# A two-branch attention kernel: products of the first branch by exact pieces of heads, narrower denominators, and a last half row in two quarters

## The chip, the cores and the metric

The kernel runs on one core of a Trainium2 chip. The metric is device time in microseconds (us): 316.14 us as the median of 3 runs (315.89 to 316.18). Engines are named as the profile names them: PE (matrix products) and PEld (its weight loads), DVE (vector), ACT (scalar functions), POOL (the general engine), SP (which mostly issues DMAs).

## The reference

Two attention branches over the same 2048 x 640 input are mixed by a gate for each token. There are 32 heads of 20 columns.

```python
g = sigmoid((x * gate_w).sum(-1, keepdims=True))
# branch A: linear attention, per head h (Dh = 20)
q, k, v = split(x @ wqkv)
phi(t)  = concat(softmax(t @ w_phi[h]), softmax(-(t @ w_phi[h])))      # 40 features
kv, z   = phi(k)^T v, sum over tokens of phi(k)
a       = (phi(q) kv / (phi(q) z + 1e-6)) @ wo
# branch B: softmax attention within 4 segments of 512 tokens (lower triangle), with a
# memory M, z carried from segment to segment; o = sig(beta) * memory + (1 - sig(beta)) * softmax part
b       = o @ wo_B
return g * a + (1 - g) * b
```

## The kernel before

Everything below has an order written out by hand for all engines: the emission order in the code is the order of each engine's queue. Tokens go in 16 chunks of 128 (`ch` or `sc`, 0 to 15), the 640 columns of a projection in KC = 5 blocks `j` of 128. A block of 128 columns doesn't end where a head of 20 does: heads 6, 12, 19 and 25 lie across two blocks.

The stages, in order of time:

1. Start, to about 9 us. The weight for keys of branch A is multiplied by the feature weight `w_phi`: `emit_foldT` turns block `ic` of the natural weight into `WkT`, and `emit_foldM` (L183) multiplies it by `Wphi`, a table that holds, for each block `j`, the feature weights of the heads `TH[j]`, each masked to the rows of the block that belong to the head. `emit_Wphi` builds the five tables on DVE and POOL. ACT copies each result to `WkA`.
2. Keys and values of branch A, to about 52 us: for each chunk `pk`, its two exponentials (`Ek`), the sums and reciprocals (`ksum`, `krec`), the normalized features `EkSn` (POOL, and DVE for the last), and `vA`.
3. The fold of the query weight (`WqA`, again `emit_foldM`, five times) at 53 to 57 us, then `kv` (L391) for each block `j`, which `emit_kvn` masks and writes into `kvn`, and the sums `z` by additions on DVE. `kvd` holds for each block two columns a head: the sum's entries, and ones of the mask.
4. Queries of branch A, 61 to 88 us: `emit_pq` makes `pq` and ACT the two exponentials `Eq` (signs `sgn` 0 and 1) in two halves `qb` of 1024 tokens. `emit_first_den` makes the denominators of chunks 0 to 3.
5. The products, 88 to 126 us. A loop over chunks and signs takes 32 groups. `emit_num` (L471) makes one group in a PSUM tile of two banks (heads 0 to 15 and 16 to 31), from one of three buffers taken in turn: `nps[(2 * ch + sgn) % 3]`. `PIECES` lists its matmuls as (block j, bank, first head, last head + 1); all of a group's matmuls write into one tile, where those in `FIRST` open a bank and those in `LAST` close it. DVE multiplies the group by the reciprocal sums (`emit_tt`, L524), POOL adds the two signs (L683, `oA`, from `tt` tiles of which there are two), and SP turns the sum for the output projection. Between groups PE runs one half projection of branch B (`emit_half`, L606, matmuls at L554, evicted by ACT at L613). Where `ch % 4 == 1` for chunks 1, 5 and 9, `emit_den` (L489) makes the denominators of two chunks behind each sign's group, 20 matmuls, in free columns of the same tile; DVE reads them at L500 and L501, and from there on POOL prepares the next four chunks' factors (L515, L517).
6. Branch B, 126 to 303 us: bursts of scores (L754), exponentials on ACT (`PT`, L758), triangles on POOL (L765), products with V (L808), with the remaining projections and the output products spread among them by `PLAN`.
7. The end, from 303 us: the output rows of chunks 12 to 15, in halves of 320 columns called (n, half). `fill` (L1058) and `turned_mm` multiply the turned blocks by WoB; `evict` (L1108) either adds the row so far on DVE (for halves in `SUMMED`) or copies on ACT, and issues the output DMA named in `out_to`. The half (2, 1) comes last: it takes the bank of half (0, 0) when ACT has copied that one, and has five matmuls, an add on DVE and a DMA on SP.

The groups in PSUM are opened by the first matmul of a bank; later matmuls of the same bank write columns that nothing has written since, or add to those that something has.

The lists that the change replaces:

```python
TH = [(0, 12), (6, 13), (12, 25), (19, 26), (25, 32)]
PIECES = [(0, 0, 0, 12), (2, 0, 12, 16), (2, 1, 16, 25), (4, 1, 25, 32),
          (1, 0, 6, 13), (3, 1, 19, 26)]
FIRST, LAST = {0, 2}, {4, 5}
HW = 13
```

Blocks 0 and 2 are taken over heads to which they have no rows (7 to 11, and 20 to 24), where their tables hold zeros. In columns a group is 240, 80, 180, 140, 140 and 140, in all 920.

Of the kernel before, what the change touches and what calls it, by code (L numbers as in the profile page):

```python
# [8 lines left out]
ALU = mybir.AluOpType  # L9
# [6 lines left out]
def kernel(  # L16
# [15 lines left out]
    nc = tc.nc  # L32
    P = 128
    S = 2048
    D = 640
    H = 32
    DH = 20
    KC = D // P
# [7 lines left out]
    out2 = out[0]  # L46
# [10 lines left out]
    bd01 = const.tile([P, 4], F32, name="bd01")  # L57
    EPS_HI = 1.0 / 2 ** 20 + 3.0 / 2 ** 26
    epsm = const.tile([P, 4], F32, name="epsm")
    TH = [(0, 12), (6, 13), (12, 25), (19, 26), (25, 32)]  # L60
    PIECES = [(0, 0, 0, 12), (2, 0, 12, 16), (2, 1, 16, 25), (4, 1, 25, 32),
              (1, 0, 6, 13), (3, 1, 19, 26)]
    FIRST, LAST = {0, 2}, {4, 5}
    HW = 13

    gS = res.tile([P, NCH], F32, name="gS")
    omgS = res.tile([P, NCH], F32, name="omgS")
# [31 lines left out]
    for what in "w1 w3 x0 g v0 v1".split():  # L99
        n = int(what[1:]) if len(what) > 1 else 0  # L100
# [17 lines left out]
    for g in range(3):  # L118
# [16 lines left out]
                            compare_op=ALU.is_ge, fill=0.0, base=DH - 1, channel_multiplier=-1)  # L135
    wmw = Aw.tile([P, KC, HW], F32, name="wmw")
    nc.gpsimd.memset(wmw, 0.0)
    Wphi = wq_hold.tile([P, KC, HW, DH], BF16, name="Wphi")
    kvn = Aw.tile([P, 2, KC, HW, DH], BF16, name="kvn")
    kvd = Aw.tile([P, 2, KC, H, 2], BF16, name="kvd")  # L140
    for j, (h0, h1) in enumerate(TH):
        nc.gpsimd.tensor_copy(out=wmw[:, j, 0:h1 - h0], in_=wmask[:, j, h0:h1])
    def emit_Wphi(j, eng):
        h0, h1 = TH[j]
        eng.tensor_tensor(out=Wphi[:, j, 0:h1 - h0, :],
                                in0=Wc[:, j:j + 1, :].to_broadcast([P, h1 - h0, DH]),
                                in1=wmask[:, j, h0:h1, None].to_broadcast([P, h1 - h0, DH]),
                                op=ALU.mult)

    for j, eng in ((0, nc.vector), (4, nc.gpsimd), (2, nc.vector), (1, nc.gpsimd), (3, nc.gpsimd)):  # L150
        emit_Wphi(j, eng)
    for sgn in range(2):
        nc.gpsimd.memset(kvn[:, sgn], 0.0)
# [10 lines left out]
    for row, val in ((DH, EPS_HI), (DH + 1, 1e-6 - EPS_HI)):  # L164
        nc.gpsimd.affine_select(out=epsm, in_=epsm, pattern=[[-32, 4]], compare_op=ALU.not_equal,
                                fill=val, base=-row, channel_multiplier=1)
# [6 lines left out]
    def w2tile(name):  # L173
        return aps.tile([P, 2, 512], F32, name=name, tag="w2")
# [8 lines left out]
    def emit_foldM(WT, dst, ic, eng=nc.scalar.copy):  # L183
        ps = w2tile("fold_ps")
        for n, (j, bk, lo, hi) in enumerate(PIECES):
            h0 = TH[j][0]
            nc.tensor.matmul(ps[:, bk, (lo - 16 * bk) * DH:(hi - 16 * bk) * DH],
# [129 lines left out]
    for step in "T0a T2d M0a T1d M2a T4d M1a T3d X0 M4a M3a k0 g k1 v0 v1 r0 r1".split():  # L317
        n = int(step[1:2] or 0)
# [26 lines left out]
    for n in range(KC):  # L345
# [12 lines left out]
        out=xg, in0=vA[:, :, 0, 320].rearrange("p (g u) -> p u g", u=4)[:, :, :, None].to_broadcast([P, 4, 4, 4]),  # L358
        in1=bd01[:, None, None, :].to_broadcast([P, 4, 4, 4]), op=ALU.mult)
# [42 lines left out]
    def emit_kvn(j):  # L402
        h0, h1 = (P * j) // DH, (P * j + P - 1) // DH + 1
        g0 = TH[j][0]
        nc.vector.tensor_tensor(
# [24 lines left out]
    for what in "z4 f0 g0 f1 f2 f3 g1 l0 l1 n0 n1 z1 g2 l2 n2 z1 g3 l3 n3 q0 f4 g4 l4 z9 n4 h0 e0".split():  # L430
        j = int(what[1:])
# [31 lines left out]
    WoB = WvA.rearrange("p c b n -> p (c b n)")[:, 0:KC * D].rearrange("p (c n) -> p c n", c=KC)  # L463
# [7 lines left out]
    def emit_num(ch, sgn):  # L471
        qb, qc = divmod(ch, HB // P)
        t = nps[(2 * ch + sgn) % 3].tile([P, 2, 512], F32, name="num")
        for n, (j, bk, lo, hi) in enumerate(PIECES):
            h0 = TH[j][0]
            nc.tensor.matmul(t[:, bk, (lo - 16 * bk) * DH:(hi - 16 * bk) * DH],  # L476
# [12 lines left out]
    def emit_den(t, ch):  # L489
        qb, qc = divmod(ch, HB // P)  # L490
        for sgn in range(2):
            for j in range(KC):
                nc.tensor.matmul(t[:, sgn].rearrange("p h e -> p (h e)"),  # L493
                                 lhsT=Eqs[qb, j][:, sgn, qc * P:(qc + 1) * P],
                                 rhs=kvd[:, sgn, j].rearrange("p h e -> p (h e)"),
                                 start=(j == 0), stop=(j == KC - 1))

    def emit_rr(rr, uu, t, o, n):
# [73 lines left out]
    def emit_first_den():  # L572
        for n in range(NB):
            emit_den(dt[:, n], n)
# [67 lines left out]
    def emit_num_at(i):  # L642
        if i < len(order):
            ch, sgn = order[i]
            t = nums[ch, sgn] = emit_num(ch, sgn)
            if ch % 4 == 1 and ch < NCH - 4:
                for n in range(2):
                    emit_den(den_view(t)[:, n], ch + 3 + 2 * sgn + n)
# [6 lines left out]
    for ch in range(NCH):  # L655
# [4 lines left out]
        for sgn in range(2):  # L660
            t = nums.pop((ch, sgn))
# [12 lines left out]
            if (ch, sgn) in EXPS:  # L674
                part = EXPS[ch, sgn]
                nc.scalar.activation(out=(phiks[1][:, 0] if part == "k" else phiq_st)[:, :, 0:DH],
                                     in_=stages[part][0][:, :, 0:DH], func=ACT.Exp)
            if (ch, sgn) in TWICE:
                emit_next_half()
            if ahead and k == 2 and sgn == 0:  # L680
# [3 lines left out]
                                in0=tt[:, 0], in1=tt[:, 1], op=ALU.add)  # L684
# [19 lines left out]
    with ExitStack() as bctx:  # L704
# [11 lines left out]
        def st_tile():  # L716
            st_pools.append(st_pools.pop(0))
            return st_pools[-1].tile([P, 2, L], F32, name="st_ps")

        oBs, ogs = {}, {}  # L720
        nda = bnd.tile([P, 2, 512], F32, name="nda")
# [140 lines left out]
        oTs, rows = {}, {}  # L862
# [112 lines left out]
        oT4 = oTA[:, 0:4]  # L975
# [42 lines left out]
        first = NCH - 4  # L1018
        oB = oBs[NSEG - 1]
        pair_ps = [st_tile() for _ in range(2)]  # L1020
        banks = {(n, half): pair_ps[n][:, half, 0:320] for n in range(2) for half in range(2)}

        def row_mm(n, half):
            nc.tensor.matmul(banks[n, half], lhsT=ident_b,
                             rhs=rows[first + n][:, half * 320:(half + 1) * 320], start=True, stop=False)
# [27 lines left out]
                tdv = td[:, :, ji].rearrange("p n (j i) d -> p n j i d", j=2)  # L1053
                nc.vector.tensor_tensor(out=oview[:, j:j + 2], in0=tdv[:, 0], in1=tdv[:, 1], op=ALU.add)

        SUMMED = {(0, 1), (1, 1), (3, 0), (2, 1)}

        def fill(n, half, k5s):  # L1058

            own = (n, half) not in SUMMED  # L1060
            if own:
                row_mm(n, half)
            for k5 in k5s:
                nc.tensor.matmul(banks[n, half], lhsT=oT4[:, n, k5, :],
                                 rhs=WoB[:, k5, half * 320:(half + 1) * 320],
                                 start=(k5 == 0 and not own), stop=(k5 == KC - 1))
# [28 lines left out]
        def last_tr(n):  # L1095
# [7 lines left out]
        last_tr(3)  # L1103
        nc.scalar.copy(out=oT4[:, 2:4, 4, :], in_=tp[:, 2:4])
        out_to = {(0, 1): (nc.sync, 0, 0), (1, 1): (nc.sync, 1, 0), (2, 0): (nc.sync, 2, 0),
                  (3, 1): (nc.scalar, 3, 0), (2, 1): (nc.sync, 2, 320)}

        def evict(n, half):  # L1108
            row = rows[first + n][:, half * 320:(half + 1) * 320]
            if (n, half) in SUMMED:  # L1110
                nc.vector.tensor_tensor(out=row, in0=banks[n, half], in1=row, op=ALU.add)
            else:
                nc.scalar.copy(out=row, in_=banks[n, half])
            if (n, half) in out_to:
                eng, n, lo = out_to[n, half]
                hs = slice(lo, (half + 1) * 320)
                eng.dma_start(out=out2[(first + n) * P:(first + n + 1) * P, hs], in_=rows[first + n][:, hs])

        both = ((0, 0), (0, 1), (1, 0), (1, 1)), ((2, 0), (3, 0), (3, 1))
# [4 lines left out]
            turned_mm(n, half, (4,))  # L1124
        for n, half in both[0]:
            evict(n, half)
        banks[2, 1] = pair_ps[0][:, 0, 0:320]
        fill(2, 1, range(KC))
        for n, half in both[1] + ((2, 1),):
            evict(n, half)  # L1130


# [28 lines left out]
```

## Time and profile before

| what | value |
|---|---|
| median of 3 runs | 316.14 us (315.89 to 316.18) |
| the profiled execution's own time | 315.77 us |
| its span, first to last instruction | 314.1 us |
| granted PE clock | 1.000 |
| PE busy | 304.0 us, 97% |
| ACT busy | 252.2 us, 80% |
| DVE busy | 223.7 us, 71% |
| POOL busy | 209.0 us, 67% |
| matmuls | 4014, each with a weight load |

The profile is of one execution, and its durations stand against that execution's time; the 1.67 us between span and time lie outside the instructions. A busy time is the sum of what an engine's instructions took. A matmul's duration there includes the way through the array (a matmul of 64 columns shows 0.193 us, though the next starts 0.029 us later), so what a matmul costs in a row of matmuls is read from start to start, which is how the chain of waits counts it. The chain follows what ended last back through its releasers, so an engine can carry the chain all through a stage and still be tied with another one.

### The profile page before, as it was taken

How to read it: one execution, taken by the hardware profiler on the slowest of the kernel's cores; microseconds unless marked ns; L12 is line 12 of the kernel's file. 1: busy time of each engine (PE TensorE's matmuls, PEld its weight loads, DVE VectorE, ACT ScalarE, POOL GpSimd, SP SyncE). 2: the span in 40 equal slices, each digit the busy share in tenths (PEclk: the TensorE clock that was granted, in tenths of full speed). 3: DMA queues.
4: the chain of work that ended last, by engine and by line, in shares of the span. 5: the costliest groups of instructions: out<-in, count | busy, mean ns of one | idle time of the engine just before them, and what ended most of it. 6: DMA issues, size and time to landing. Idle time of an engine off the chain costs nothing.

```text
span 314.1 us, 9759 instructions
## 1 busy us (share of the span) xinstructions
PE 304.0 (97%) x4014; PEld 208.3 (66%) x4014; DVE 223.7 (71%) x507; ACT 252.2 (80%) x320; POOL 209.0 (67%) x308
## 2 busy tenths in 40 slices
PE   8999999999999999999999999999999999999995
PEld 7788877755578888465566666665656666665673
DVE  3487997999779997568767586877755765445463
ACT  4677888277845648999998999999998898998953
POOL 8788599004247989856657477878786877666550
DMA  7988934439137979755221583386653453222132
GB/s 208 211 183 201 220 97 135 120 105 366 57 19 139 140 111 140 152 93 89 51 55 33 69 144 64 74 111 68 88 107 76 90 93 73 66 75 55 45 92 84
DMA packets 94006, 34.55 MB, mean 110 GB/s; under 512 B 82442, under 2 KB 93834, under 8 KB 93962
## 3 DMA queue, kind: packets, MB, share of 16 engines
q1 hardware_dynamic: 93386, 33.28, 52.6%
q10 hardware_dynamic: 576, 0.66, 0.8%
q8 instruction: 31, 0.51, 0.7%
q14 instruction: 13, 0.11, 0.1%
HBM read 6.10 MB, written 2.62 MB: 28 GB/s over the span
## 4 chain that ended last, share of the span: by engine, by line
PE 73%; ACT 22%; DMA 2%; issue 1%; DVE 1%; ACTq 0%; DVEq 0%
ACT PT L758 19%; PE st_ps L754 9%; PE proj L884 9%; PE proj L940 9%; PE pk L240 7%; PE pq L418 7%; PE proj L554 7%; PE pv L240 7%; PE nda L808 6%; PE num L476 4%; PE kv_ps L391 2%; DMA wnat_k<-in_A_wqkv_dram 2%; PE num L493 1%; PE nda L816 1%; ACT ek L912 1%
## 5 line engine op out<-in xcount | busy, mean ns | idle before, releaser
L758 ACT ACTIVATE PT<-st_ps 128x1024 bf16<-128x1024 f32 x160 | 153.7, 1023 | 12.7 <-PE st_ps L754 10.4
L765 POOL TENSOR_SCALAR_AFFINE_SELECT PT<-PT 128x512 bf16<-128x512 bf16 (+1 forms) x130 | 87.0, 688 | 45.7 <-ACT PT L758 45.4
L808 PEld LDWEIGHTS <-PT 128*128 128x128 bf16 x1280 | 40.0, 96 | 9.5 <-issue 5.6
L808 PE MATMUL nda<-vB,PT 128*128 128x21 bf16 x1240 | 41.6, 173 | 0.1
L259 POOL TENSOR_TENSOR EkSn<-Ek,krec 128x1280 bf16<-128x1280 bf16 x15 | 35.1, 2360 | 7.9 <-DVE krec L258 6.0
L946 DVE CAST Z<-proj 128x320 bf16<-128x320 f32 x44 | 21.1, 488 | 23.5 <-PE proj L940 22.4
L940 PEld LDWEIGHTS <-xTf 128*128 128x128 bf16 x300 | 26.4, 97 | 14.2 <-issue 5.7
L425 ACT ACTIVATE Eq<-pq 128x1024 bf16<-128x1024 f32 x20 | 19.4, 1021 | 12.0 <-PE pq L418 12.0
L255 DVE TENSOR_REDUCE ksum<-Ek 128x64 f32<-128x1280 bf16 x16 | 23.6, 1475 | 7.2 <-ACT Ek L251 7.2
L524 DVE TENSOR_TENSOR tt<-num,rr 128x640 f32<-128x640 f32 x32 | 25.0, 814 | 4.5 <-POOL rr L517 1.7
L884 PE MATMUL proj<-WkA,oTA 128*128 128x320 bf16 x160 | 28.2, 300 | 0.0
L683 POOL TENSOR_TENSOR oA<-tt 128x640 bf16<-128x640 f32 x16 | 24.6, 1541 | 5.2 <-DVE tt L524 5.0
L754 PE MATMUL st_ps<-Z 32*128 32x512 bf16 (+3 forms) x256 | 24.7, 299 | 3.2 <-ACT PT L758 2.3
L251 ACT ACTIVATE Ek<-pk 128x640 bf16<-128x640 f32 x32 | 20.8, 703 | 7.9 <-PE pk L240 6.8
L754 PE MATMUL st_ps<-Eq 32*128 32x512 bf16 (+3 forms) x256 | 25.1, 299 | 1.9 <-ACT PT L758 1.3
L240 PEld LDWEIGHTS <-xTf 128*128 128x128 bf16 x200 | 22.6, 113 | 4.7
L848 POOL TENSOR_TENSOR oB<-td 128x320 bf16<-128x320 f32 x22 | 19.0, 861 | 5.0 <-DVE td L845 5.0
L418 PE MATMUL pq<-xTf,WqA 128*128 128x512 bf16 x100 | 22.2, 379 | 0.0
L884 PE MATMUL proj<-WvA,oT 128*128 128x320 bf16 x120 | 21.0, 300 | 0.0
L845 DVE TENSOR_TENSOR td<-nda,rec 128x640 f32<-128x640 f32 x23 | 19.0, 825 | 2.5 <-DVE rec L835 0.5
L554 PEld LDWEIGHTS <-xTf 128*128 128x128 bf16 x180 | 16.2, 97 | 4.6
L884 PEld LDWEIGHTS <-oTA 128*128 128x128 bf16 x160 | 13.6, 97 | 8.0 <-issue 4.0
(178 smaller groups left out, 554.2 us busy)
## 6 DMA issues: line engine op xcount, KB each, us to landing
Z<-EkSn SPq DMA_DIRECT2D x32, 160.0 KB, 2.9
out_dram<-orow SPq DMA_DIRECT2D x8, 160.0 KB, 1.8
out_dram<-oTA SPq DMA_DIRECT2D x6, 160.0 KB, 1.8
WvA<-in_A_wqkv_dram SPq DMA_DIRECT2D x2, 400.0 KB, 6.3
WvB<-in_B_wv_dram SPq DMA_DIRECT2D x1, 800.0 KB, 4.7
WkB<-in_B_wk_dram SPq DMA_DIRECT2D x1, 800.0 KB, 6.5
WqB<-in_B_wq_dram SPq DMA_DIRECT2D x1, 800.0 KB, 8.2
WkA<-in_A_wo_dram SPq DMA_DIRECT2D x1, 800.0 KB, 9.9
```

The costliest lines, as they stand in the source:

```text
L240: nc.tensor.matmul(ps[:, bk, 0:n], lhsT=key_tokens(c, sc), rhs=rhs, start=(c == 0), stop=(c == by_row[-1][0] if sc == 0 and W is WkA else ...
L259: (nc.vector if sc == NCH - 1 else nc.gpsimd).tensor_tensor(out=EkSn[:, sc].rearrange("p s (h f) -> p (s h) f", f=DH), in0=Ek.rearrange("p ...
L418: nc.tensor.matmul(pq[:, half, :], lhsT=WqA[:, c, j * P:(j + 1) * P], rhs=xq[:, 2 * qb + half, c], start=(c == 0), stop=(c == KC - 1))
L524: nc.vector.tensor_tensor(out=tt[:, sgn].rearrange("p (b h) d -> p b h d", b=2), in0=ps, in1=csb, op=ALU.mult)
L554: nc.tensor.matmul(ps, lhsT=xq[:, sc // 4, cc, sc % 4 * P:(sc % 4 + 1) * P], rhs=W[:, cc, half * 320:(half + 1) * 320], start=(cc == 0), s ...
L683: nc.gpsimd.tensor_tensor(out=oA.rearrange("p (h d) -> p h d", d=DH), in0=tt[:, 0], in1=tt[:, 1], op=ALU.add)
L754: nc.tensor.matmul(ps[:, i - i0, o:o + L - c * P], lhsT=kT[32 * i:32 * i + 32, c * P:(c + 1) * P], rhs=qT[32 * i:32 * i + 32, c * P:L], st ...
L758: nc.scalar.activation(out=PT[:, i0:i0 + 2], in_=ps, func=ACT.Exp, scale=SCALE_B)
L765: nc.gpsimd.affine_select(out=v, in_=v, pattern=[[0, n_i], [1, P]], compare_op=ALU.is_ge, fill=0.0, base=0, channel_multiplier=-1)
L808: nc.tensor.matmul(nd[:, j, i], lhsT=block(st, c)[:, i, (j - c) * P:(j - c + 1) * P], rhs=vB[:, c, 4 * st.g + i, :], start=(c == 0), stop= ...
L884: nc.tensor.matmul(ps, lhsT=oT[:, k % KC], rhs=W[:, k % KC, hs], start=(k == 0), stop=(k == n - 1))
L940: nc.tensor.matmul(ps, lhsT=xq[:, sc // 4, k, sc % 4 * P:(sc % 4 + 1) * P], rhs=W[:, k, half * 320:(half + 1) * 320], start=(k == 0), stop ...
```

## The change

Three things:

1. `TH` is now the heads that have rows in block `j`: (0, 7), (6, 13), (12, 20), (19, 26), (25, 32). `PIECES` has ten pieces in order of blocks, with the shared heads 6, 12, 19 and 25 as pieces of their own where a second block adds to them, and a block that reaches over head 16 cut there. A group has ten matmuls of 140, 20, 120, 20, 60, 80, 20, 120, 20 and 120 columns, in all 720. The tables `Wphi`, `kvn` and `wmw` are 8 heads wide and not 13, which makes the memsets and products that fill them smaller, and the tables of `Wphi` are built in order of blocks.
2. In `emit_den` block 0 still writes all 32 heads (64 columns), and blocks 1 to 4 write only their own heads: 14, 16, 14 and 14 columns.
3. Half (2, 1) is no longer filled and evicted as a whole. Its columns 320 to 479 go to the bank of half (0, 0) and 480 to 639 to that of half (1, 0), in five matmuls of 160 columns each; after the other evictions DVE adds the two quarters, and one DMA on SP writes out columns 320 to 639 as before.

```diff
-    TH = [(0, 12), (6, 13), (12, 25), (19, 26), (25, 32)]
-    PIECES = [(0, 0, 0, 12), (2, 0, 12, 16), (2, 1, 16, 25), (4, 1, 25, 32),
-              (1, 0, 6, 13), (3, 1, 19, 26)]
-    FIRST, LAST = {0, 2}, {4, 5}
-    HW = 13
+    TH = [(P * j // DH, (P * j + P - 1) // DH + 1) for j in range(KC)]
+    PIECES = [(0, 0, 0, 7), (1, 0, 6, 7), (1, 0, 7, 13), (2, 0, 12, 13), (2, 0, 13, 16),
+              (2, 1, 16, 20), (3, 1, 19, 20), (3, 1, 20, 26), (4, 1, 25, 26), (4, 1, 26, 32)]
+    FIRST, LAST = {0, 5}, {4, 9}
+    HW = 8
...
-    for j, eng in ((0, nc.vector), (4, nc.gpsimd), (2, nc.vector), (1, nc.gpsimd), (3, nc.gpsimd)):
+    for j, eng in ((0, nc.vector), (1, nc.gpsimd), (2, nc.vector), (3, nc.gpsimd), (4, nc.gpsimd)):
         emit_Wphi(j, eng)
...
             for j in range(KC):
-                nc.tensor.matmul(t[:, sgn].rearrange("p h e -> p (h e)"),
+                lo, hi = TH[j] if j else (0, H)
+                nc.tensor.matmul(t[:, sgn, lo:hi].rearrange("p h e -> p (h e)"),
                                  lhsT=Eqs[qb, j][:, sgn, qc * P:(qc + 1) * P],
-                                 rhs=kvd[:, sgn, j].rearrange("p h e -> p (h e)"),
+                                 rhs=kvd[:, sgn, j, lo:hi].rearrange("p h e -> p (h e)"),
                                  start=(j == 0), stop=(j == KC - 1))
...
-        SUMMED = {(0, 1), (1, 1), (3, 0), (2, 1)}
+        SUMMED = {(0, 1), (1, 1), (3, 0)}
...
-                  (3, 1): (nc.scalar, 3, 0), (2, 1): (nc.sync, 2, 320)}
+                  (3, 1): (nc.scalar, 3, 0)}
...
-        banks[2, 1] = pair_ps[0][:, 0, 0:320]
-        fill(2, 1, range(KC))
-        for n, half in both[1] + ((2, 1),):
+        quarters = [(pair_ps[0][:, 0, 0:160], 320), (nda[:, 0, 0:160], 480)]
+        for ps, lo in quarters:
+            for k5 in range(KC):
+                nc.tensor.matmul(ps, lhsT=oT4[:, 2, k5, :], rhs=WoB[:, k5, lo:lo + 160],
+                                 start=(k5 == 0), stop=(k5 == KC - 1))
+        for n, half in both[1]:
             evict(n, half)
+        row = rows[first + 2]
+        for ps, lo in quarters:
+            nc.vector.tensor_tensor(out=row[:, lo:lo + 160], in0=ps, in1=row[:, lo:lo + 160], op=ALU.add)
+        nc.sync.dma_start(out=out2[(first + 2) * P:(first + 3) * P, 320:640], in_=row[:, 320:640])
```

## The prediction

> **What bounds the kernel now.** I read the chain of waits first, then single stages. In the fences ahead of the last, columns are start (or total) and duration in us. The page's share by engine:
>
> ```profile
> PE 73%; ACT 22%; DMA 2%; issue 1%; DVE 1%; ACTq 0%; DVEq 0%
> ```
>
> PE carries the end, except where ACT's exponentials do (from 126 us on, and the fold of WqA at 52 to 57 us). All edits but the last lie before 126 us. The chain over the stage of the first branch's products (88 to 126 us) alternates two groups, `num` and a projection, with denominators (L493) among them:
>
> ```profile
> 88.31 0.80 PE num L476 x12
> 89.11 1.36 PE proj L554 x10
> ...
> 90.90 0.58 PE num L493 x20
> ...
> 114.89 0.68 PE proj L554 x5
> 115.57 0.42 PE num L476 x6
> 115.99 0.68 PE proj L554 x5
> 116.67 0.40 PE num L476 x6
> ```
>
> So the stage looks like PE alone; cheaper `num` groups should be worth their whole saving. The one 0.42 among the 0.40s made me ask who follows PE. The waits of 86 to 126 us (total, times, longest):
>
> ```profile
> POOL oA L683 <- DVE tt L524: 5.0, 3, 2.4
> DVE rr L500 <- PE z_den L493: 2.2, 1, 2.2
> DVE tt L524 <- POOL rr L517: 1.7, 3, 0.6
> DVE tt L524 <- POOL oA L683: 1.2, 1, 1.2
> DVE tt L524 <- PE num L493: 1.2, 1, 1.2
> ```
>
> DVE waits for PE only at the head: for the first denominators at 84.9 us, `num` 0 at 88.8 us (0.4 us), and `num` 2 with its denominators at 91.59 us. After that it waits only for POOL, and POOL for DVE: a DVE and POOL chain that a faster PE can't speed up. And PE depends on it: three `num` buffers, so group i+3 overwrites what DVE reads of group i. The timeline at that 0.42:
>
> ```profile
> 115.09 0.29 DVE L501 TENSOR_TENSOR uu<-num,rr 128x128 f32<-128x128 f32 x1
> 115.28 0.53 PEld L476 LDWEIGHTS <-Eq 128*128 128x128 bf16 x6
> 115.30 0.81 DVE L524 TENSOR_TENSOR tt<-num,rr 128x640 f32<-128x640 f32 x1
> 115.43 0.56 PE L476 MATMUL num<-kvn,Eq 128*128 128x240 bf16 x6
> ```
>
> DVE's last read of group 19's buffer ends at 115.38 and PE writes group 22 at 115.43: PE already waited 0.02 us there. From the single records, such handovers leave, beyond the 0.05 us that the semaphore takes, 0.10 us at group 14, 0.14 at 17, 0 at 22, 0.03 at 25, 0.09 at 27 and 0.10 at 31, the last. PE and DVE are tied.
>
> **Part 1, pieces.** From start to start, single records show 102 ns for a matmul of 240 columns, 79 for 180, 60 or 61 for 140 (63 before another line's), 35 for 80. With 320 at 136 that is 2.5 ns plus 0.417 ns a column. Before: 102+35+79+61+61+63 = 400 ns. For narrow ones, with full 128x128 weight loads:
>
> ```profile
> 303.69 0.99 PE st_ps L808 x40
> ```
>
> 25 ns at 21 columns; four of 12 columns (L364) and of 4 (L367) also pace at 25, and 64 columns (L493) at 0.58/20 = 29. So the ten pieces (20 columns a head) cost 7 heads 61, 1: 25, 6: 52, 1: 25, 3: 28, 4: 35, 1: 25, 6: 52, 1: 25, 6: 52, sum 380 ns: 20 ns less, though four instructions more. A one-head piece after a wide one isn't in the trace: between 11 ns (its columns by the line above) and the 35 of 80 columns a group could gain 76 or lose 20. I take 25, as the rows of 21 and of 12 columns, the nearest, with the same loads.
>
> The Trainium skill (TensorE: Matmul & The Clock Gate, section Back-to-back issue gap) speaks against splitting: it says a sustained stream of load and matmul pairs costs about 81 ns each at 128 columns. By that a group would go from 486 to 810 ns. The 25 ns at 21 columns and 400 ns for six pieces disagree.
>
> 32 groups: 0.64 us of PE. The fold uses the same list. Of K's five folds, two lie ahead of PE's wait for a weight DMA at 6.67 us; three follow, and ACT's evictions between them and `pk` (0.62 us idle <- PE fold_ps) pass on two: 0.04 us, after which PE is unbroken. Q's five are hidden by ACT evicting WqA until 56.9 us (0.67 us each against 0.40): nothing.
>
> **Part 2, denominators.** Per chunk 8 of 10 matmuls go from 64 to 14 or 16 columns, 29 to 25 ns: 0.032 us. The first four chunks, 83.6 us: 0.13. Twelve more: 0.38.
>
> **What passes.** Up to DVE's wait at 91.59 us PE gains 0.04+0.13, three groups 0.06, two chunks of denominators 0.06: 0.29 us, and DVE and POOL start 0.29 earlier. What PE saves later it can keep only as far as the handovers leave room: 0.29 ahead at group 22 and 0.29+0.10 = **0.39 at group 31**. Of 1.19 us (0.64+0.51+0.04), 0.8 turns into PE waiting for DVE. With pairs 2 ns cheaper or dearer the same walk gives 0.49 or 0.23. Behind PE's wait stand only the next projections; ACT evicts those 0.65 us idle at 125.3 and moves with PE.
>
> **Set-up work.** Smaller `kvn` memsets (2 x 1.18 us for 1300 elements, now 800: 0.9 us of POOL) end before 8 us; POOL's first product at 14.24 us waits 1.60 us for DVE's `krec` anyway. Narrower `Wphi` on DVE (0.66 and 0.64 us) and its new order on POOL (last at 5.22): the first fold starts when ACT has copied WkT, 5.22, and needs piece 4 about 0.3 later. All nothing; without that cover, some 0.1. The second section then runs on ACT's PT; its first PT, bank frees and POOL's triangles move by 0.29 to 0.39, and I pass on 0.39.
>
> **Part 3, the last half row.** Before: five matmuls 309.94 to 310.78, DVE add 310.82 to 311.31 (0.49), output DMA 311.33. Two quarters: 10 x 69 ns, the same 0.69. DVE is free at 310.49, just when quarter one is done; quarter two's add (0.33, the row of 128x160 at L1054) runs 310.83 to 311.16. The DMA goes out 0.15 earlier. Quarter two's bank was read last by DVE at 310.05, before it is wanted at 310.28. But the windows of the end (before the last two numbers: clock; last two: DMA share, GB/s):
>
> ```profile
> 310.50:311.00 0.50, 0.28 (x3) 0.00 (x0) 0.18 (x1) 0.12 (x1) 0.00 (x0) 1.00 0.91 317
> 311.00:311.50 0.50, 0.00 (x0) 0.00 (x0) 0.31 (x1) 0.00 (x0) 0.00 (x0) 1.00 0.95 321
> 311.50:312.00 0.50, 0.00 (x0) 0.00 (x0) 0.00 (x0) 0.00 (x0) 0.00 (x0) 1.00 0.97 309
> 312.00:312.50 0.50, 0.00 (x0) 0.00 (x0) 0.00 (x0) 0.00 (x0) 0.00 (x0) 1.00 0.98 336
> ```
>
> All DMA engines are full from the first output packet to the last, with 0.02 to 0.05 of each half us free. The last 80 KB, issued earlier, queue behind the same bytes. Between 0 and 0.15 I take 0.05, near what is free.
>
> **Sum.** 0.39+0.05 = 0.44 off the profiled execution's 315.77 us (span 314.1 and 1.67 around it): 315.33. That execution lies 0.37 under the median 316.14, so by the median's scale 315.7.
>
> **Rivals.**
> A: everything passes. If PE wins its 1.19 and the tail 0.15, 1.34 off: 314.8. For it: PE fills the whole chain. Against: the handovers. In part (a POOL or DVE step that I call fixed moves too) anything over 0.63 us off. Together 0.24.
> B: it is slower. A narrow pair between wide ones costs more than 25 ns because its load can't run ahead behind so short a matmul. At 30 ns a `num` group gains nothing, and past 29 a denominator loses. At 35: 32 x 0.020 + 16 x 0.048 = 1.4 us, on PE with no cover: 317.5. Against: 25 ns at three widths. 0.10.
> C: a load is not hidden behind a short matmul at all and is paid in full, 98 ns in its own row (L476 and L493, PEld): 32 x (4 x 0.073 - 0.020) + 16 x 8 x 0.069 = 17.5 us, so 333. The 25 ns rows, with the same loads, all but exclude it: 0.01. The TensorE page's 81 ns a pair, of the Trainium skill, is a rule of this kind.
> D: the earlier gain is lost in the second section (DVE's or POOL's later buffers set it), leaving 0 to 0.2: 316.0. Too little to tell from the forecast by a time: 0.10.
>
> **Numbers.** The forecast holds 0.55, with its own range 315.3 to 316.0. The range of 8 in 10 takes in A's end and the dear end of the narrow price: 314.9 to 316.6. A measurement of this kernel tells about 0.2%, 0.63 us, from no change. Faster by more: A, 0.24. Within: forecast and D, 0.65. Slower: B and C, 0.11.
>
> **What would show it.** Right: `num` groups of ten at 0.38, denominators at 0.52 per 20 in the free stretches, and at groups 14, 17, 22 and 25 a PE wait for DVE's reads, with DVE's own rows 0.3 earlier; the first PT near 126.4; the last add near 0.33; DMA still full after 310 us. Wrong: no such waits and DVE 0.8 earlier at 124 us (A), or narrow pairs over 29 ns (B).

## The result: slower by a quarter of a per cent

| | before | after |
|---|---|---|
| median of 10 runs, us (lowest to highest) | 315.96 (315.63 to 316.27) | 316.75 (316.50 to 317.36) |
| ratio after/before, 95% interval | | 1.0026 [1.0016, 1.0035] |
| profiled execution, us (span) | 315.77 (314.1) | 316.55 (314.8) |
| granted clock, mean | 1.000 | 0.999 |

The forecast was 315.7 with a range to 316.6, 0.44 us off the time. It came out 0.79 us over: a sign that I had given 0.11. The stage that I had worked on hardest did what was forecast. What was lost is in the tail, priced as a small gain, and perhaps near 61 us, priced at nothing.

### The profile page after: what moved, and what is told of

It is laid out like the page before. It is cut to its first block, busy times and chain, and to the rows that moved or that the text cites. A ratio compares the mean times of both kernels' runs of the same rounds, so it can differ in the third digit from the quotient of the medians.

```text
span 314.8 us, 10102 instructions
## 1 busy us (share of the span) xinstructions
PE 303.3 (96%) x4183; PEld 208.0 (66%) x4187; DVE 223.5 (71%) x508; ACT 252.2 (80%) x320; POOL 207.8 (66%) x308
## 4 chain that ended last, share of the span: by engine, by line
PE 67%; ACT 22%; DVE 6%; POOL 2%; issue 2%; ACTq 0%; DVEq 0%; POOLq 0%
ACT PT L761 19%; PE st_ps L757 9%; PE proj L887 9%; PE proj L943 9%; PE pk L242 7%; PE pq L420 7%; PE pv L242 7%; PE nda L811 6%; PE proj L557 3%; DVE tt L527 2%; PE num L478 2%; DVE rr L503 2%; PE kv_ps L393 2%; POOL oA L686 1%; PE nda L819 1%
```

## The profile after

The page's share of the chain of waits by engine, and the row of queue 8 from its DMA queues (packets, MB, share):

```profile
q8 instruction: 33, 0.54, 0.7%
...
PE 67%; ACT 22%; DVE 6%; POOL 2%; issue 2%; ACTq 0%; DVEq 0%; POOLq 0%
```

PE has lost 6 points of the chain, DVE has won 5 and POOL 2. Queue 8 stood at 31 packets, 0.51 MB before: two more. What that row carries is told below.

**The products.** The chain from 88 to 127 us (start, duration):

```profile
90.73 0.45 PE num L478 x10
91.18 0.52 PE num L496 x20
...
115.26 0.30 DVE uu L504
115.56 0.04 issue
115.61 0.54 PE num L478 x10
116.15 0.68 PE proj L557 x5
116.83 0.38 PE num L478 x10
```

A `num` group of ten takes 0.38 us (0.40 with six), twenty denominators 0.52 (0.58): the forecast prices. And the chain now passes through DVE's `uu` to reach group 22 at 115.61. The waits of 86 to 126 us (total, times, longest):

```profile
DVE tt L527 <- POOL rr L520: 1.7, 3, 0.6
DVE tt L527 <- POOL oA L686: 1.2, 1, 1.2
...
PE num L478 <- DVE uu L504: 0.2, 1, 0.2
```

The two waits of DVE for POOL are as long as before, the last row is new, and so is group 22's place in the timeline:

```profile
115.26 0.29 DVE L504 TENSOR_TENSOR uu<-num,rr 128x128 f32<-128x128 f32 x1
...
115.61 0.54 PE L478 MATMUL num<-kvn,Eq 128*128 128x140 bf16 x10 [0.21 <-DVE uu L504]
```

From the end of the ninth of the ten pairs of query exponentials (85.60 us before) to the first PT, this execution is 0.38 us shorter than before's; 0.35 was forecast for that stretch (0.39 less 0.04 of the fold, which lies ahead of it). The tenth pair, behind the first denominators, ends 0.13 nearer to the ninth: the forecast's 0.13 for the first four chunks.

**A stop near 61 us.** The `kv` products and the query projections, PE's rows alone of the timeline, before and then after:

```profile
58.83 1.97 PE L391 MATMUL kv_ps<-vA,EkSn 128*64 128x80 bf16 x98
60.73 2.33 PE L418 MATMUL pq<-xTf,WqA 128*128 128x512 bf16 x10
```

```profile
60.92 0.39 PE L420 MATMUL pq<-xTf,WqA 128*128 128x512 bf16 x1
61.59 1.90 PE L420 MATMUL pq<-xTf,WqA 128*128 128x512 bf16 x8 [0.28 <-issue]
```

Between two projections that nothing holds back, PE stops: "issue" means that it waited for nothing that the profile shows. One of the ten projections has no record here (1 and 8 are shown), so the stop is shorter than the rows look: 0.25 us reach the first query exponentials.

**The loss at the end.** The timeline after 309 us, before and then after (SPq and ACTq are the queues' issues):

```profile
309.68 1.99 SPq L1117 DMA_DIRECT2D out_dram<-oTA  x4
```

```profile
309.74 2.31 SPq L1120 DMA_DIRECT2D out_dram<-oTA  x3
...
310.89 0.32 DVE L1139 TENSOR_TENSOR oTA<-nda,oTA 128x160 bf16<-128x160 f32 x1
312.15 0.41 SPq L1140 DMA_DIRECT2D out_dram<-oTA  x1
```

The last add ends at 311.21, but its DMA leaves at 312.15, behind three others that took 2.31 us. By line (lowest, median, highest ns of one):

```profile
L1120 SPq DMA_DIRECT2D out_dram<-oTA x3: 332/397/1401, 309.7 to 311.7; - x3
```

One issue took 1.40 us; before, the four took 0.33 to 0.40. While SP stands in it, the DMA engines run dry: the windows of the end (the last two numbers are DMA share and GB/s):

```profile
310.50:311.00 0.50, 0.35 (x6) 0.15 (x3) 0.48 (x3) 0.18 (x1) 0.00 (x0) 1.00 0.77 279
311.00:311.50 0.50, 0.00 (x0) 0.00 (x0) 0.21 (x1) 0.00 (x0) 0.00 (x0) 1.00 0.14 33
311.50:312.00 0.50, 0.00 (x0) 0.00 (x0) 0.00 (x0) 0.00 (x0) 0.00 (x0) 1.00 0.84 292
```

A share of 0.14 where before had 0.95. And the DMA queues of 309.5 to 315 us have a row that the same window of before lacks:

```profile
q8 instruction: 1, 0.02, 1.1%
```

**Sum.** Marks of after against the same marks of before: the first key exponentials +0.18, the end of the ninth pair of query exponentials +0.43, the first PT +0.05, the last PT +0.05, the end +0.78. So +0.18 at the start, +0.25 at 61 us, -0.38 in the products, +0.73 in the tail.

**What queue 8 carries.** The profile calls it "instruction", and its packets follow PE's program: one of 16384 bytes per some 255 of PE's matmuls and loads (8028 of them and 31 packets before, 8374 and 33 after). I call such a packet a fetch. The change adds 32 x 4 pieces in the products, 10 x 4 in the folds and 5 in the tail, each a weight load and a matmul: 256 + 80 + 10 = 346 instructions, one block of 256 and 90 over. So the block borders fall elsewhere, and so do the moments of the fetches: the last at 304.42 us before, at 310.18 (for 0.99 us) after. SP's second output DMA, the slow one, was issued at 310.16 and ended at 311.56, 0.40 behind the fetch. SP's transposes show the same tie: from 62 us on, in both traces, 23 of the 37 that overlap a fetch took over 1.4 us, up to 2.5, and none of the 116 that overlap no instruction packet took over 1.3.

## The experiments

My theory after the result: the pieces gain what was forecast, and the 90 instructions over a whole block cost more than that, by the place of PE's fetches. Rivals: the quarters of the tail themselves cost it (a DMA behind their adds, or banks), or the narrow pieces do, or the start of the execution. Comparisons are with the kernel before on the same chip; marks are shifts against the profile of before, and "the products" runs from the ninth pair of query exponentials to the first PT.

**Changed kernel again.** No edit.

> The changed kernel again, on the same chip as the next three. Theory 1 (instruction fetch): PE's 346 added instructions move the places where PE's next 16 KB of code is fetched; one such fetch, on DMA queue 8, starts near 310.2 us and holds the second output DMA on SP for 1.0 us, so the last output DMA leaves near 312.15 and not 311.2. It shows again here: about 0.7 us over the kernel before (ratio 1.002 to 1.003). Theory 2 (the quarters): the last DMA is late because of the two quarter adds and their waits; same time. The slow granted clock until 6.85 us, 0.18 us at the start, may or may not come again: if it comes, the change makes it.

316.66 us, ratio 1.0022 [1.0013, 1.0032]. The products -0.35; near 61 us two projections stand 0.96 us apart from start to start, where 0.22 is usual, and the mark is at +0.73; a fetch at 310.21, an output DMA of 1.59 us, and +0.95 in the tail. The start came out at -0.10 here against +0.18 in the first trace: in the ten traces of this section it lies anywhere from -0.37 to +0.85, so the +0.18 can't be put down to the change.

**Sixty idle instructions added to after, ahead of everything.**

```diff
-    for n in range(25):
-        nc.tensor.matmul(warm[n % 2][:, 0, 0:P], lhsT=zero_b, rhs=zero_b, ...)
+    for n in range(55):
+        nc.tensor.matmul(warm[n % 2][:, 0, 0:58], lhsT=zero_b, rhs=zero_b[:, 0:58], ...)
```

> The changed kernel with 60 more PE instructions ahead of everything: the 25 warm-up matmuls of 128 columns become 55 of 58 columns, the same time on the cold clock. Theory 1: the last fetch comes 60 instructions earlier, some 2 us, near 308 us, when SP has nothing to issue; the last DMA leaves near 311.2 and the span falls by 0.7 to 1.0 us against the changed kernel: ratio to before 0.997 to 1.000. Theory 2: nothing changes, ratio 1.002 to 1.003.

316.13 us, 1.0008 [0.9998, 1.0018]: sixty instructions more, and 0.14% less time. The last fetch is at 306.70, SP's issues take 0.33 to 0.41 us, and last PT and end are both at +0.79: the tail's loss is gone, with the quarters in place. The products keep -0.35. But the gap near 61 us grew to 1.13 from start to start:

```profile
61.15 0.71 PE L393 MATMUL kv_ps<-vA,EkSn 128*64 128x80 bf16 x28 [0.93 <-issue]
```

**Ninety idle instructions added to before, at the same place** (70 matmuls of 46 columns, the same edit).

> The kernel before with 90 more PE instructions ahead of everything (70 warm-up matmuls of 46 columns for the 25 of 128), which is 346 less one block of 256. Nothing of the change is in it. Theory 1: a fetch near 310 us that the kernel before hasn't, an SP output DMA of 1.3 to 1.4 us in place of 0.35, and 0.5 to 1.0 us more: ratio 1.0015 to 1.003. Theory 2: no difference (within 0.15 us).

319.07 us, 1.0091 [1.0071, 1.0111]: far slower, but not where I had expected it. The tail lost nothing: no fetch after 304.08. One loss is a gap of PE near 60.5 us (+1.58)

```profile
62.06 0.26 PE L391 MATMUL kv_ps<-vA,EkSn 128*64 128x80 bf16 x3 [1.37 <-issue]
```

and the other a wait of PE at 90 us, for ACT's last query exponentials:

```profile
89.87 1.94 ACT L425 ACTIVATE Eq<-pq 128x1024 bf16<-128x1024 f32 x2 [1.46 <-PE pq L418]
91.86 0.56 PE L476 MATMUL num<-kvn,Eq 128*128 128x240 bf16 x6 [1.63 <-ACT Eq L425]
```

ACT isn't late by itself: both exponentials stand at +1.52, as PE's projections ahead of them do. What differs is who waits for them. In the kernel before, group 1 starts 0.40 us behind group 0, and group 2 starts 0.05 behind the end of these exponentials. Here it is group 1 that starts 0.05 behind that end, 2.19 us behind group 0. So the edit also changed which group waits for ACT, why isn't shown, and these 1.79 us are no cost of the place of instructions. At most the 1.58 are. Nor does the count alone say where the last fetch falls: this kernel has 4059 matmuls, as many as the one with forty-five late ones below, but 31 packets to its 32 and no fetch in the tail.

**The fold alone put back to six pieces** (own lists `FOLD6`, `TH6` and a `Wphi` 13 heads wide for it; products, denominators and quarters as in after: 266 instructions more than before, 10 over a block).

> The changed kernel with the fold of the weights as before (six pieces, tables 13 heads wide); products, denominators and quarters as changed. PE has 80 instructions fewer than the changed kernel, 10 more than a whole block over the kernel before. Theory 1: no fetch at the end and no stall of PE near 61 us; what the products and denominators pass on (0.35 us: the 0.39 of the prediction without the fold's 0.04) is kept, and the tail gives up to 0.1: 0.35 to 0.5 us under the kernel before, ratio 0.9984 to 0.9990. Theory 2: the last DMA stays late, ratio 1.000 to 1.002.

315.70 us, 0.9993 [0.9983, 1.0003], some 0.3% under after. No stall near 61 us (+0.01), no fetch after 304.13, the tail 0, the products -0.35. Ten pieces in the fold were to gain 0.04; without the 80 instructions in them the kernel takes about 1 us less.

**Denominators alone.**

```diff
+                lo, hi = ((0, 32), (6, 13), (12, 20), (19, 26), (25, 32))[j]
-                nc.tensor.matmul(t[:, sgn].rearrange("p h e -> p (h e)"),
+                nc.tensor.matmul(t[:, sgn, lo:hi].rearrange("p h e -> p (h e)"),
```

> The kernel before with the denominators narrowed and nothing else: not one PE instruction more or fewer, so no fetch of code moves. Theory 1 with the tie to DVE: 0.13 us from the first four chunks and 0.06 from the two chunks ahead of DVE's first free run reach DVE, and the handover's 0.10 at the last group adds to them: 0.29 us of the 0.51 that PE saves, ratio 0.9991. Rival A (all of it passes): 0.51, ratio 0.9984. Rival B (narrow ones are dearer): 1.000 or more. In the profile: 20 denominators in 0.51 to 0.52 us, and the first PT 0.29 earlier against the last query exponentials.

315.75 us, 0.9990 [0.9980, 1.0001]. The products' stage gained 0.21, where 0.29 was expected. Near 61 us this kernel had a gap of 0.52 us from start to start (+0.52), though not one instruction ahead of it had moved.

**Products and denominators, without the rest** (the kernel with the six-piece fold, and the last half row undivided as before: exactly 256 instructions more).

> The kernel before with the ten-piece products and the narrow denominators, but the fold of six pieces and the undivided last half row: PE has 256 instructions more, one block of code exactly, so the fetches fall where they fell. Tie: 0.35 us less, ratio 0.9989, no stall at 61 us, no fetch after 305 us, end as the last PT. Rival A: 1.15 us less, ratio 0.9964. Theory 2 (it was the quarters) agrees with the tie here.

315.59 us, 0.9982 [0.9973, 0.9991]: faster than both kernels. The products -0.36, the tail 0, its four output issues 0.33 to 0.40 us.

**Quarters alone.** The tail of the change, on before: 10 instructions more.

> The kernel before with the last half row in two quarters and nothing else (10 PE instructions more, 14 short of the next fetch's place). Theory 1 with full DMA engines: the last add ends and the last DMA leaves 0.15 us earlier, the end comes 0.00 to 0.05 earlier; ratio 0.9998 to 1.0000. Theory 2: last DMA 0.9 us late, ratio 1.0025. Rival (DMA engines not the bound): end 0.15 earlier.

316.00 us, 0.9991 [0.9979, 1.0003]. From the last PT on, the last DMA leaves 0.15 us earlier, as forecast, and the end comes 0.01 earlier: the DMA engines are full until then (shares of 0.94 to 0.98 from 311 to 313 us).

```profile
311.30 0.33 DVE L1136 TENSOR_TENSOR oTA<-nda,oTA 128x160 bf16<-128x160 f32 x1
311.65 0.33 SPq L1137 DMA_DIRECT2D out_dram<-oTA  x1
```

```profile
L1117 SPq DMA_DIRECT2D out_dram<-oTA x3: 332/383/403, 310.2 to 311.1; - x3
```

This add is followed by its DMA at once, where after's waited 0.94 us; the quarters are no cause of the loss.

**The four one-head pieces left out** (with the six-piece fold; this leaves out those heads' part of the first branch's products).

```diff
         for n, (j, bk, lo, hi) in enumerate(PIECES):
+            if hi - lo == 1:
+                continue
```

> The six-piece-fold version of e4 with the four one-head pieces left out of every product group (parts of the first branch's products are then missing): PE is relieved of another 4 x 25 ns in each of 32 groups, 3.2 us, and has one block of code less than e4. Tie to DVE: groups 0 and 1 are hidden behind ACT's last query exponentials, group 2 gives 0.10 to DVE, so the first PT moves by 0.41 us in place of 0.35, ratio 0.9987; the rest is PE waiting for DVE. Rival A (PE alone bounds the stage): 3.5 us, ratio 0.989.

315.53 us, 0.9984 [0.9974, 0.9994]. PE is relieved of another 32 x 4 x 25 ns = 3.2 us, and the stage gains 0.57 against 0.35. The rest is PE waiting:

```profile
PEld L485 <- issue: 4.1, 9, 0.9
...
PE num L485 <- DVE uu L511: 1.4, 2, 0.7
...
PE num L485 <- DVE tt L534: 0.8, 4, 0.3
```

So the tie to DVE is real, and what the narrow pieces themselves cost is nearly all hidden. I had expected 0.41; where the other 0.16 comes from, no run says.

**Thirty idle matmuls in after, late** (at about 130 us, 4 columns each: 60 instructions behind the `kv` stretch, ahead of the tail).

```diff
                 burst()
+                if dstep == 0 and n == 2:
+                    for _ in range(30):
+                        nc.tensor.matmul(nda[:, 1, 0:4], lhsT=ident_b, rhs=ident_b[:, 0:4], ...)
```

> The changed kernel with 30 idle matmuls of 4 columns (60 PE instructions) put in at about 130 us, where ACT sets the pace. What lies before 130 us is the changed kernel's own, the wait for code near 61 us included. Theory 1: the last fetch of code moves from 310.2 to about 307 to 308 us, all SP output DMAs take 0.3 to 0.4 us, and the 0.7 to 0.95 us between the last exponential and the end are gone: 0.7 to 0.9 us under the changed kernel, ratio to before 0.9990 to 1.0005. Rival (the tail is late for another reason): ratio 1.002 to 1.003.

317.16 us, 1.0037 [1.0024, 1.0051]. I had expected the idle matmuls to be hidden; the stretch at 133 to 135 us became 1.24 us longer, so the total missed. The tail did as expected: the last fetch at 307.33, last PT +1.30, end +1.29, and the last DMA directly behind its add.

```profile
310.99 1.30 SPq L1123 DMA_DIRECT2D out_dram<-oTA  x3
...
312.13 0.33 DVE L1142 TENSOR_TENSOR oTA<-nda,oTA 128x160 bf16<-128x160 f32 x1
312.49 0.33 SPq L1143 DMA_DIRECT2D out_dram<-oTA  x1
```

**Forty-five of them in before** (90 instructions, at the same place).

> The kernel before with 45 such idle matmuls (90 PE instructions) at about 130 us: nothing of the change, and nothing ahead of 130 us moved. Theory 1: a fetch begins between 309.5 and 311 us and holds an output DMA on SP for 1.0 us; 0.5 to 0.95 us between the last exponential and the end, ratio 1.0015 to 1.003. If the fetch falls just behind the last issue, nothing is lost, and the last line of the fetches says so. Rival: no difference but what 45 matmuls cost at 130 us (at most 1.1 us there, seen before the last exponential).

317.62 us, 1.0049 [1.0031, 1.0066]. The stretch at 133 to 135 us became 1.22 us longer, as with thirty, so it isn't the idle matmuls' own time alone. On top the tail has after's loss, with nothing of the change in the kernel: a fetch at 310.84, SP's second output DMA, issued at 311.18, takes 1.35 us, and from the last PT to the end +1.06 becomes +1.74: 0.68 us.

```profile
310.75 2.76 SPq L1120 DMA_DIRECT2D out_dram<-oTA  x4
```

```profile
L1120 SPq DMA_DIRECT2D out_dram<-oTA x4: 332/399/1353, 310.8 to 313.1; - x4
```

The last two runs and the sixty-instruction pad are the proof for the tail: moving the fetch away removes the loss from after, moving one in puts it into before.

## Why the prediction was wrong, step by step

- **Part 1, price of a piece: right.** 25 to 27 ns for one head behind a wide one, 27 for three heads, 35 for four, 51 to 52 for six, 60 to 61 for seven: 0.38 a group. (The six terms of before add to 401 ns, not 400; nothing hangs on it.) Rival B (over 29 ns) and C fall. The Trainium skill (TensorE: Matmul & The Clock Gate, section Back-to-back issue gap) has 81 ns a pair at 128 columns; these rows disagree.
- **Part 2, denominators: right in the price** (25 ns at 14 and 16 columns, 0.52 per twenty). Alone they gave 0.21 where 0.29 was expected; no run says which 0.08 is lost.
- **What passes: right.** 0.35 to 0.38 for 0.35 in the six traces with the ten pieces. The waits stand at two of the places named, groups 14 and 22 (the 0.54 in the chain at 105.69 and 115.61), and rival A (all of the 1.19) falls with the run that relieves PE of 3.2 us more and gains 0.2. The stage keeps it to the end: D falls too, since last PT and first PT shift alike. One part of the walk was wrong: I let groups 0 and 1 pass on their 2 x 0.02 us, but group 2 is held by ACT. Its last query exponentials end at 88.64 + 1.94 = 90.58, and group 2 starts 0.05 behind them, as it did before (90.29 and 90.34):

```profile
88.64 1.94 ACT L427 ACTIVATE Eq<-pq 128x1024 bf16<-128x1024 f32 x2 [1.46 <-PE pq L420]
...
90.63 0.54 PE L478 MATMUL num<-kvn,Eq 128*128 128x140 bf16 x10
```

Without these 0.04 the walk gives 0.31, and it missed by 0.08 in the run with denominators alone and by 0.16 in the one without one-head pieces. That the ten pieces came out at 0.35 is in part luck.

- **Part 3, the quarters: right by themselves.** 0.15 earlier, and 0.01 at the end for the 0.05 that I took.
- **The step that failed is the price of the added instructions.** I counted each new piece by its 25 ns on PE and stopped there: "four instructions more" were part of a sum of column times. In this kernel they also move the fetches of PE's program, and those were priced at nothing because I never asked what queue 8 was. In the tail a fetch came to lie on an output DMA of SP, and that cost 0.73 and 0.95 in the two traces of after. So "the DMA goes out 0.15 earlier" turned into 0.82 later, 312.15 against 311.33, and the DMA engines were no longer full: the cover that made the quarters worth nothing was broken from another side. None of the four rivals held this.
- **Set-up: "nothing" is right for what I listed**, POOL's and DVE's work. The fold's 0.04 can't be told apart at a start that varies by more.
- **The sum by the runs:** -0.35 in the products, 0.73 to 0.95 in the tail, and near 61 us some 0.25, +0.6 to +0.85 in all; the medians differ by 0.79.

**What stays open.** The stretch near 61 us. Its cost is +0.25, +0.73 and +0.52 in the three traces with after's count of instructions up to there, mean 0.50, and 0 to 0.52, mean 0.26, in the seven where that count is before's. The means differ by 0.24, but the two sets overlap and single executions of one code differ, so how much of it the change brings is not settled. It is larger in the two runs with idle instructions ahead of everything (1.13 and 1.58), but no run moved a fetch there alone. Not known either is why the run with ninety idle instructions ahead has no fetch in its tail. Nor is it settled whether quarters on top of products and denominators cost anything: 0.9993 with them, 0.9982 without, and the intervals overlap.

## What to carry to other kernels

Count the instructions that an edit adds to an engine, not only their durations: where the program is fetched in blocks, an edit in one stage moves the fetches of every later one. Then read in the trace where the fetches fell, since the count alone did not always tell it here. An edit worth some tenths of a per cent is judged only when it is also run with the count put back to the same place in a block: here the products and denominators of a change that measured 1.0026 measured 0.9982, with the fold and the last half row left as they were and exactly one block of instructions added.

## What the runs showed of the hardware

- PE's program comes in pieces of 16384 bytes, one per some 255 of its rows. The Trainium skill (Runtime: NRT & Kernel Launch, section Instruction fetch mechanics) gives the same 16 KiB and 256 instructions, and calls the cost of crossing a border "mostly hidden". The traces agree on the size; the second fails in the tail, where 0.68 to 0.95 us were not hidden.
- A DMA issue on SP that meets such a fetch can take about 1 us longer. Of the output DMAs that overlap one in the twelve traces, three did, all in the tail (1.35 to 1.59 us, each ending 0.40 or 0.41 behind the fetch); the other 26 kept their 0.33 to 0.35. Of the transposes from 62 us on, 138 of 241 that overlap one took over 1.4 us, and one of 670 that overlap no instruction packet. What sets the held ones apart isn't known.
- In the `kv` stretch and just behind it, PE stopped with nothing shown to wait for in eight of the twelve traces, 0.2 to 1.6 us each, and each stop ended 2.2 to 3.0 us after a fetch had begun. 256 of its short instructions last about 3.0 us there. That PE ran out of instructions is the likely reading; no run shows it, and the other four traces have a fetch at this place and no stop over 0.04.
- The granted clock's release at the start (transposes of 128 columns going from 107 to 56 ns) came anywhere from 3.9 to 7.0 us in the twelve traces, about 5.5 in before and 6.8 in after. The first key exponentials don't simply follow it: with a release at 4.9 us they were 0.85 late (PE had waited 1.11 us for a weight DMA), with one at 7.0 only 0.40.
